# Polysketch attention and hash routing on one core: an earlier end of the early class, gathers ahead of the last x, and a last group in column parts

## The chip, the core and the metric

The kernel runs on one core of one Trainium2 chip. The metric is device microseconds of one execution. The kernel before took 229.28 us as the median of three runs (229.06 to 229.42).

## What is computed

An attention block is followed by a mixture of experts, whose expert for each row follows from the row's token id. All data are float32.

```
q, k, v: (4 batches, 4 heads, 1088 positions, 32);  S1, S2: (8, 32)
phi(x)  = outer product of S1 x and S2 x, 64 features
kv      = sum over positions of phi(k) outer v;   z = sum of phi(k)
attn    = (phi(q) kv) / (phi(q) z + 1e-6)
x       = attn, rows (batch, position), 4352 rows of 4 * 32 = 128
expert  = token_id * 2654435761 mod 8
out     = relu(x w1[expert]) w2[expert],  w1: (8, 128, 1024), w2: (8, 1024, 128)
```

## The kernel before

**Attention, one batch after another.** In a batch, the first 1024 positions are laid out as 128 partitions by T = 8 positions; the last 64 of each batch are handled as tails, all batches together. For batch b, TensorE (PE) transposes k (`transposed`), multiplies by the sketches (`k_products`, `q_products`), and sums kv over the positions (`kv_products`). VectorE (DVE) forms the features: `k_features` (tile kp) from the copied products ab, and `q_features` (tiles f, then fT, its transposed form) in two halves of four positions each, g = 0 and 1. ScalarE (ACT) copies products out of PSUM (`copied`) and puts kv into a block-diagonal matrix m with 16 small copies (`kv_diagonal`, L383). `x_products` multiplies the q features by m in eight groups of matmuls per half, and ACT copies the result to xe. `x_tail_products` does the same for the tail. `denominators` and `x_rows` divide: the main rows on GpSimd (POOL) mostly, one half of one batch on DVE. SyncE (SP) then stores the rows to a scratch tensor x_rows in DRAM, a main store and a tail store for each batch. The loop is skewed: in turn b, the products and kp of batch b + 1 are made between kv and x of batch b, and k of batch b + 2 is transposed.

**The routing**, spread over the turns on DVE: `route_counts` and `route_ranks` count rows for each expert, `route_slots` gives each row its slot, `route_rows` and `route_tiles` make one-hot matrices (row, in_tile, tiles; one half of tiles is made on POOL, L286), and `route_list` and `route_end` turn them, by 34 small matmuls into one PSUM tile, into the row lists `get` and `put`. Each expert has two classes of GN = 288 slots. The early class takes the first 288 rows of the expert among rows 0 to NE - 1, where NE covers the first EB = 3 batches (3264 rows); the late class takes the rest of the expert's rows. What exceeds both classes is done by a loop at the end, whose number of turns is read from n_over.

**The experts**, in 16 groups (8 early, then 8 late) of 288 slots. `bring` gathers tiles of 128 rows by indirect DMA on POOL (L537; six buffers xg), transposes them on PE three at a time, and copies them to xT. `layer1` (L601) has eight matmuls of 288 columns per group, each copied out with a relu by ACT and DVE in turn; `layer2` (L609) has eight, which add up, and runs one group behind. `send` transposes results back and scatters them by indirect DMA on POOL (L542). A gather of an early tile reads only rows below NE, so it waits for the stores of those rows only.

**What sets the order.** Through attention the order on every engine is the order of the program text (`manual_schedule`), up to `ordered.close()`. After it a scheduler places the instructions. In both parts each engine works its list in order. An issued gather waits on POOL, and what stands behind it on POOL waits too. In the last turn of attention before, ten matmuls on constants (`keep_busy(10)`, L157) stand between kv and x:

```python
        if not more:
            keep_busy(10)
        x_products(fTs, m)
        x_tail_products(b, m)
```

The scheduler placed eight gathers ahead of the last batch's x rows on POOL, and `bring` of the first six tiles ahead of the first `layer1`. It placed the last scatter behind the load of n_over and the loop.

Of the kernel before, what the change touches and what calls it, by code (L numbers as in the profile page):

```python
# [24 lines left out]
def kernel(  # L25
# [31 lines left out]
    EB = B - 1  # L57
    NE = EB * S
    EP = NE // C
# [4 lines left out]
    assert E * GN % P == 0 and GN >= P and ST <= P and EP * C == NE and EP % 32 == 0  # L64
# [3 lines left out]
    load = ctx.enter_context(tc.tile_pool(name="load", bufs=2))  # L68
# [27 lines left out]
    def load_main(src, b, tag):  # L96
        t = load.tile([P, H, T, D], F32, tag=tag, name=f"{tag}{b}")
        nc.sync.dma_start(t[:], src[b, :, :SM, :].rearrange("h (p t) d -> p h t d", t=T))
        return t

# [181 lines left out]
    def route_tiles():  # L282
        nc.vector.tensor_tensor(in_tile[:], iota[:, 0:ST].unsqueeze(1).to_broadcast([P, C, ST]),
                                st[:, 0].unsqueeze(2).to_broadcast([P, C, ST]), op=OP.is_equal)
        nc.vector.tensor_scalar(tiles[:, :, 0], in_tile[:], p1[:], None, op0=OP.mult)  # L285
        nc.gpsimd.tensor_tensor(tiles[:, :, 1], in_tile[:], iota[:, 0:C].unsqueeze(2).to_broadcast([P, C, ST]),  # L286
                                op=OP.mult)
# [28 lines left out]
    xe = const.tile([P, GQ * H * Q + H, DA], F32)  # L316
# [21 lines left out]
    def copied(ab_ps, sub):  # L338
        ab = work.tile(list(ab_ps.shape), F32, tag="ab", name="ab")
        nc.scalar.copy(sub(ab), sub(ab_ps))  # L340
        return ab
# [73 lines left out]
    def x_products(fTs, m):  # L415
        for g, fT in enumerate(fTs):
            for h0 in range(0, H, 2):
                p = ps_x.tile([P, 2, Q * DA], F32, tag="x", name="x_ps")
                for h in range(2):
                    for fb in range(FB):  # L420
                        nc.tensor.matmul(p[:, h], fT[:, (h0 + h) * FB + fb],  # L421
                                         m[:, h0 + h, fb].rearrange("p t d -> p (t d)"),
                                         start=(fb == 0), stop=(fb == FB - 1), skip_group_check=True)
                nc.scalar.copy(xe[:, (g * H + h0) * Q:(g * H + h0 + 2) * Q].rearrange("p (h t) d -> p h (t d)", h=2), p[:])  # L424

    def x_tail_products(b, m):
        u, t = b % 2, b // 2
        rows, r = slice(u * SP, (u + 1) * SP), slice(t * D, (t + 1) * D)
        p = ps_x.tile([P, H, DA], F32, tag="x", name="x_ps")
        for h in range(H):  # L430
            for fb in range(FB):
                nc.tensor.matmul(p[rows, h], fT_tail[r, h * FB + fb, rows], m[r, h, fb, t],
                                 start=(fb == 0), stop=(fb == FB - 1), skip_group_check=True,
                                 tile_position=(r.start, rows.start))
        nc.scalar.copy(xe[rows, GQ * H * Q:], p[rows])

    def denominators():
        den = work.tile([P, GQ * H * Q + H], F32, tag="den", name="den")
        nc.vector.tensor_scalar(den[:], xe[:, :, D], 1e-6, None, op0=OP.add)
        nc.vector.reciprocal(den[:], den[:])  # L440
        return den

    def x_rows(b, den):
        u = b % 2
        xs = work.tile([P, T, H, D], F32, tag="xs", name="xs", bufs=1)
        n = H * Q
        for g in range(GQ):
            (nc.vector if b == EB - 1 and g == 0 else nc.gpsimd).tensor_tensor(xs[:, g * Q:(g + 1) * Q].rearrange("p t h d -> p h t d"),  # L448
                                    xe[:, g * n:(g + 1) * n, 0:D].rearrange("p (h t) d -> p h t d", h=H),
                                    den[:, g * n:(g + 1) * n].rearrange("p (h t) -> p h t", h=H).unsqueeze(3)  # L450
                                    .to_broadcast([P, H, Q, D]), op=OP.mult)
        rows = slice(u * SP, (u + 1) * SP)
        xs_tail = work.tile([P, H, D], F32, tag="xs_tail", name="xs_tail", bufs=1)
        nc.gpsimd.tensor_tensor(xs_tail[rows], xe[rows, GQ * n:, 0:D],
                                den[rows, GQ * n:].unsqueeze(2).to_broadcast([SP, H, D]), op=OP.mult)
        nc.sync.dma_start(x_dram[b * S:b * S + SM].rearrange("(p t) d -> p t d", t=T),
                          xs[:].rearrange("p t h d -> p t (h d)"))
        nc.sync.dma_start(x_dram[b * S + SM:(b + 1) * S], xs_tail[rows].rearrange("p h d -> p (h d)"))
# [10 lines left out]
    nc.gpsimd.memset(xe[:, GQ * H * Q:], 1.0)  # L469
# [16 lines left out]
    for b in range(B):  # L486
        more = b + 1 < B
        kv = kv_products(b, (kp, va), (kp_tail, va_tail))
        if more:
            abk_ps = k_products(kTs, T)  # L490
            abq_ps = q_products(qT, T)
            va = values(v_t[b + 1], T, work, "")
# [3 lines left out]
        if b == 1:  # L496
            route_rows(0)
        if b == 2:
            route_tiles()
        m = kv_diagonal(b, kv)  # L500
        if more:
            abk = copied(abk_ps, lambda t: t[:])
            abq = copied(abq_ps, lambda t: t[:])
            kp = k_features(abk, T, work, "")
# [3 lines left out]
        if not more:  # L508
            keep_busy(10)
        x_products(fTs, m)  # L510
        x_tail_products(b, m)
        if b + 2 < B:
            kTs = [transposed(k_t[b + 2], g, Q) for g in range(0, T, Q)]
        den = denominators()
        x_rows(b, den)
        if b == 2:
            route_end(route_list())
        if more:
            fTs = [q_features(abq, 0, slice(0, P), work, "", 2)]
        if b + 2 < B:  # L520
            qT = q_blocks(q_t[b + 2], T)
        if more:
            fTs.append(q_features(abq, 1, slice(0, P), work, "", 2))
        if b == 0:
            load_experts(range(E // 2, E))
            route_slots()
        if b == 1:
            route_rows(1)
    ordered.close()

    hots.release()
    moe = ctx.enter_context(tc.tile_pool(name="moe", bufs=3))

# [6 lines left out]

    def scatter(src, idx):
        st_ = nc.gpsimd.indirect_dma_start(  # L542
            out=out[:], out_offset=bass.IndirectOffsetOnAxis(ap=idx, axis=0),
            in_=src[:], in_offset=None, bounds_check=N - 1, oob_is_err=False)
        tc.declare_no_dep(st_.ins, group="out_rows", reason="distinct rows")
        tc.add_to_no_dep_group("out_rows", st_.ins)
# [14 lines left out]
    def columns(of, name, lo, hi):  # L561
        b = lo // (BT * P)
        if b not in of:
            of[b] = moe.tile([P, BT * P], F32, tag=name, name=name, bufs=2)
        return of[b][:, lo - b * BT * P:hi - b * BT * P]

    done_in = done_out = 0

    def bring(upto):
        nonlocal done_in  # L570
        while done_in < upto:
            n = min(3, ST - done_in)
            xp = ps_x.tile([P, 4, P], F32, tag="x", name="xp")
            for i in range(n):
                xg = moe.tile([P, DM], F32, tag="xg", name="xg", bufs=6)
                gather(xg, get[:, done_in + i:done_in + i + 1], NE if done_in + i < HT else N)
                nc.tensor.transpose(xp[:, i], xg[:], ident[:])  # L577
            evict(done_in // 3, columns(xTs, "xT", done_in * P, (done_in + n) * P),
                  xp[:, 0:n].rearrange("p a b -> p (a b)"))
            done_in += n  # L580

    def send(upto):
        nonlocal done_out
        while done_out + 1 <= upto:
            n = min(2, upto - done_out)
            tp = ps_x.tile([P, 4, P], F32, tag="x", name="tp")
            for i in range(n):
                nc.tensor.transpose(tp[:, i], columns(oTs, "oT", (done_out + i) * P, (done_out + i + 1) * P), ident[:])
# [8 lines left out]
    def layer1(g, c):  # L597
# [3 lines left out]
        nc.tensor.matmul(hp[:], w1[:, g % E, c * P:(c + 1) * P], columns(xTs, "xT", g * GN, (g + 1) * GN), start=True, stop=True)  # L601
# [4 lines left out]
    def layer2(g, c):  # L606
        if c == 0:
            ops[g] = ps_o.tile([P, GN], F32, tag="o", name="op")
        nc.tensor.matmul(ops[g][:], w2[:, g % E, c], hTs[g][:, c], start=(c == 0), stop=(c == FC - 1))  # L609
        if c == FC - 1:  # L610
            nc.scalar.copy(columns(oTs, "oT", g * GN, (g + 1) * GN), ops[g][:])  # L611

    G = 2 * E
    for g in range(G + 1):
        if g < G:
            bring(min(ST, -(-((g + 2) * GN) // P)))
        for c in range(FC):
            if g < G:
                last = layer1(g, c)
            if g > 0:  # L620
                layer2(g - 1, c)
            if c == 3 and g > 1:
                send((g - 1) * GN // P)
    send(ST)
# [4 lines left out]
    with tc.issue_after(last):  # L629
# [22 lines left out]

    w1f = w1[:].rearrange("p e f -> p (e f)")
    w2f = w2[:].rearrange("p e c d -> p (e c d)")
    turns = nc.values_load(n_over[0:1, 0:1], min_val=0, max_val=OT)
    with tc.For_i(0, turns) as j:
# [25 lines left out]
        xg = moe.tile([P, DM], F32, tag="xg", name="xg", bufs=6)  # L682
# [52 lines left out]
```

## Time and profile before

| What | us |
|---|---|
| median of three runs | 229.28 |
| the profiled execution | 229.07 |
| its span | 227.4 |
| PE busy, of the span | 203.9 |
| DVE, POOL, ACT busy | 99.1, 98.0, 70.3 |
| kv of the last batch starts on PE | 61.98 |
| first gather starts on POOL | 69.16 |
| first `layer1` matmul starts | 78.91 |
| last `layer2` matmul ends | 212.56 |
| last scatter starts | 219.61 |

How to read it: the profile is of one execution of the program, and times count from the start of its span. A busy share is no bound in itself: what counts in each stretch is which engine the others wait for. In the page's slices each digit is a tenth of a slice that the engine was busy, and PEclk is the clock that TensorE was granted, in tenths. A timeline line gives start, duration, engine, line, operation, output and inputs, shape, count, and in brackets the idle time before it with what ended it. A matmul of float32 shows as two instructions in its count.

### The profile page before, as it was taken

What the parts mean: (1) busy time and instruction counts of PE and PEld (TensorE: products, weight loads), DVE (VectorE), ACT (ScalarE), POOL (GpSimd) and SP (SyncE); (2) the same over time, 40 slices, a digit from 0 to 9 for tenths busy, and PEclk for the clock granted to TensorE, in tenths of its full rate; (3) what the DMA queues carried; (4) which work ended last, traced back from release to release, by engine and by line L of the source; (5) the groups of instructions that cost most, each with busy time, mean ns of one, the idle gap of its engine ahead of it and who ended that gap; (6) DMA issues with size and microseconds to landing.
All of it is one profiled execution on the core that took longest, in us unless ns stands there. A gap on an engine that the chain in (4) does not pass through costs nothing.

```text
span 227.4 us, 3315 instructions
## 1 busy us (share of the span) xinstructions
PE 203.9 (90%) x1172; PEld 166.1 (73%) x1173; DVE 99.1 (44%) x191; ACT 70.3 (31%) x201; POOL 98.0 (43%) x114
## 2 busy tenths in 40 slices
PE   6799889999799499999999999999999999999400
PEld 2689889999778267777777777777777777777300
DVE  4699568999994132233133212322232232324300
ACT  2243643628235123222331342232223223122100
POOL 4234017044336787046656256566265115213620
PEclk9999999999999769999999999999999999999955
DMA  4999999895021232001111001111011000000000
GB/s 123 286 311 315 314 345 347 288 344 193 3 98 30 53 121 56 16 23 38 46 35 46 23 27 46 46 35 43 19 34 45 0 22 24 15 18 21 30 20 0
DMA packets 22465, 22.16 MB, mean 97 GB/s; under 512 B 5178, under 2 KB 19771, under 8 KB 22448
## 3 DMA queue, kind: packets, MB, share of 16 engines
q1 hardware_dynamic: 17824, 17.05, 23.8%
q0 software_dynamic: 2304, 4.59, 7.0%
q10 hardware_dynamic: 2320, 0.30, 0.8%
q8 instruction: 10, 0.16, 0.3%
q14 instruction: 7, 0.06, 0.1%
HBM read 17.47 MB, written 4.59 MB: 97 GB/s over the span
## 4 chain that ended last, share of the span: by engine, by line
PE 60%; issue 13%; DMA 12%; DVE 5%; POOL 4%; ACT 2%; POOLq 1%; SPq 0%; ACTq 0%
PE hp L601 20%; PE op L609 17%; DMA out_dram<-os,put 8%; PE kv L370 7%; PE ab_ps L333 3%; POOL out_dram L542 2%; PE idle L157 2%; DMA k<-in_k_dram 2%; PE kT_ps L322 2%; PE x_ps L421 2%; PE abq_ps L398 2%; PE xp L577 1%; ACT m L383 1%; POOL xg L537 1%; DVE tiles L285 1%
## 5 line engine op out<-in xcount | busy, mean ns | idle before, releaser
L601 PE MATMUL hp<-xT,w 128*128 128x288 f32 x256 | 84.1, 416 | 0.0
L609 PE MATMUL op<-hT,w 128*128 128x288 f32 x256 | 81.9, 407 | 0.0
L552 DVE TENSOR_SCALAR hT<-hp 128x288 f32<-128x288 f32 x64 | 29.3, 458 | 89.5 <-PE hp L601 86.5
L542 POOL DMA_INDIRECT out_dram<-os,put x36 | 35.8, 993 | 59.1 <-ACT os L550 28.4
L609 PEld LDWEIGHTS op<-hT,w 128*128 128x128 f32 x256 | 48.7, 190 | 13.2
L601 PEld LDWEIGHTS hp<-xT,w 128*128 128x128 f32 x256 | 48.2, 196 | 11.5
L550 ACT ACTIVATE hT<-hp 128x288 f32<-128x288 f32 x64 | 26.3, 410 | 66.3 <-PE hp L601 62.1
L537 POOL DMA_INDIRECT xg<-x_rows,get x36 | 36.7, 1020 | 20.9 <-PE xp L577 8.7
L448 POOL TENSOR_TENSOR xs<-xe,den 128x512 f32<-128x512 f32 x7 | 9.2, 1335 | 24.1 <-DVE den L440 20.9
L383 ACT COPY m<-kv 32x66 f32<-32x66 f32 x64 | 13.2, 206 | 18.3 <-PE kv L370 17.5
L421 PE MATMUL x_ps<-m,fT 128*128 128x132 f32 x128 | 16.1, 281 | 1.5 <-ACT xe L424 1.1
L421 PEld LDWEIGHTS x_ps<-m,fT 128*128 128x128 f32 x128 | 15.0, 190 | 2.3 <-ACT xe L424 1.3
L370 PEld LDWEIGHTS kv<-va,kp 128*128 128x128 f32 x128 | 14.7, 192 | 0.4 <-issue 0.3
L370 PE MATMUL kv<-va,kp 128*128 128x66 f32 x128 | 14.9, 275 | 0.0
L611 ACT COPY oT<-op 128x288 f32<-128x288 f32 x16 | 6.4, 398 | 19.4 <-PE op L609 19.4
L412 DVE STREAM_TRANSPOSE fT<-f 128x1024 f32<-128x1024 f32 (+1 forms) x9 | 11.2, 1244 | 1.0 <-DVE f L345 0.5
L157 PE MATMUL idle<-warm 128*128 128x512 bf16 x31 | 9.8, 442 | 1.4 <-POOL warm L129 1.4
L345 DVE TENSOR_TENSOR f<-ab 128x1024 f32<-128x1024 f32 (+1 forms) x9 | 10.8, 1199 | 0.6 <-ACT ab L340 0.5
L345 DVE TENSOR_TENSOR kp<-ab 128x1024 f32<-128x1024 f32 x8 | 9.4, 1230 | 2.4 <-ACT ab L340 2.4
L577 PE MATMUL xp<-ident,xg 128*128 128x128 f32 x36 | 7.1, 290 | 3.1 <-DMA xg<-x_rows,get 1.7
L333 PE MATMUL ab_ps<-s_k,kT 128*128 128x64 f32 (+1 forms) x72 | 9.2, 277 | 0.7 <-issue 0.7
L333 PEld LDWEIGHTS ab_ps<-s_k,kT 128*128 128x128 f32 (+1 forms) x72 | 8.5, 191 | 1.6 <-issue 1.4
(133 smaller groups left out, 149.2 us busy)
## 6 DMA issues: line engine op xcount, KB each, us to landing
w<-in_moe_w_dram SPq DMA_DIRECT2D x16, 512.0 KB, 7.7
k<-in_k_dram SPq DMA_DIRECT2D x4, 512.0 KB, 4.9
q<-in_q_dram SPq DMA_DIRECT2D x4, 512.0 KB, 5.9
v<-in_v_dram SPq DMA_DIRECT2D x4, 512.0 KB, 6.3
x_rows<-xs SPq DMA_DIRECT2D x4, 512.0 KB, 4.5
xg<-x_rows,get POOLq DMA_INDIRECT x36
out_dram<-os,put POOLq DMA_INDIRECT x36
k_tail<-in_k_dram ACTq DMA_DIRECT2D x4, 32.0 KB, 5.0
```

What stands on the lines that cost most here:

```text
L157: nc.tensor.matmul(p[:], warm[:, 0:P], warm[:], start=True, stop=True)
L333: nc.tensor.matmul(ab_ps[:, g:g + w, h].rearrange("p t x r -> p t (x r)"), kT[:w * D, h], s_k[:w * D, 0:w].rearrange("p t x r -> p (t x r) ...
L345: eng.tensor_tensor(dst, ab[:, :, 0].unsqueeze(3).to_broadcast(shape), ab[:, :, 1].unsqueeze(2).to_broadcast(shape), op=OP.mult)
L370: nc.tensor.matmul(kv[:, pr], kp[rows, t, 2 * pr:2 * pr + 2].rearrange("p h i j -> p (h i j)"), va[rows, t, 2 * pr:2 * pr + 2].rearrange(" ...
L383: nc.scalar.copy(m[t * D:(t + 1) * D, h::2, f, t], src)
L421: nc.tensor.matmul(p[:, h], fT[:, (h0 + h) * FB + fb], m[:, h0 + h, fb].rearrange("p t d -> p (t d)"), start=(fb == 0), stop=(fb == FB - 1 ...
L537: nc.gpsimd.indirect_dma_start(out=dst[:], out_offset=None, in_=x_dram[0:rows], in_offset=bass.IndirectOffsetOnAxis(ap=idx, axis=0), bound ...
L542: st_ = nc.gpsimd.indirect_dma_start(out=out[:], out_offset=bass.IndirectOffsetOnAxis(ap=idx, axis=0), in_=src[:], in_offset=None, bounds_ ...
L550: nc.scalar.activation(dst, src, AF.Relu if relu else AF.Copy)
L552: return nc.vector.tensor_scalar(dst, src, 0.0, None, op0=OP.max).ins
L601: nc.tensor.matmul(hp[:], w1[:, g % E, c * P:(c + 1) * P], columns(xTs, "xT", g * GN, (g + 1) * GN), start=True, stop=True)
L609: nc.tensor.matmul(ops[g][:], w2[:, g % E, c], hTs[g][:, c], start=(c == 0), stop=(c == FC - 1))
```

## The change

1. The early class ends within batch 2: EB is 2, and NE is 2686, the two first batches and most of the first 512 rows of the third. q of that batch is loaded in two parts of 512 positions, so that each half g of it makes 512 neighbouring rows, which are stored by a DMA of their own.
2. The last two batches are written out of the loop. The list (`route_list`) comes before x of batch 2, whose first half (g = 0) stands before kv of batch 3 and whose second half and tail stand behind it. Six gathers are issued on POOL before x of batch 3, three more by the scheduler. Only three tiles are transposed ahead of the first `layer1`; `bring` moves behind the fourth matmul of each group. xe has two buffers, ab three, and xg and xT lie in a pool of their own, so that they exist before attention ends. `keep_busy(10)` is gone.
3. `route_slots` moves to turn 0, ahead of kp; `route_rows` follows x of turns 0 and 1; both halves of tiles are made on DVE. All x rows of batch 2 are made on DVE, those of batch 3 on POOL.
4. The last group's `layer2` runs as two column parts (160 and 128), with a `send` behind each. The tables of the overflow loop are made after group 12, and a barrier of the scheduler stands ahead of the loop: in the built order, the last scatter stands ahead of the load of n_over.

```diff
-    EB = B - 1
-    NE = EB * S
-    EP = NE // C
+    EB = B - 2
+    EP = (EB * S + SM // 2) // C
+    NE = EP * C
...
-        nc.gpsimd.tensor_tensor(tiles[:, :, 1], in_tile[:], iota[:, 0:C].unsqueeze(2).to_broadcast([P, C, ST]),
+        nc.vector.tensor_tensor(tiles[:, :, 1], in_tile[:], iota[:, 0:C].unsqueeze(2).to_broadcast([P, C, ST]),
...
+    b, e = EB, EB + 1
+    kv = kv_products(b, (kp, va), (kp_tail, va_tail))
+    abk_ps = k_products(kTs, T)
+    abq_ps = q_products(qT, T)
+    va = values(v_t[e], T, work, "")
+    m = kv_diagonal(b, kv)
+    abk, abq2 = copied(abk_ps, lambda t: t[:]), copied(abq_ps, lambda t: t[:])
+    kp = k_features(abk, T, work, "")
+    idx = route_list()
+    x_products(b, 0, fTs[0], m)
+    route_end(idx)
+    kv = kv_products(e, (kp, va), (kp_tail, va_tail))
+    denominators(b, 0, HQ)
+    x_main(b, 0, nc.vector)
+    fetch(3)
+    fTs.append(features_of(abq, 1))
+    x_products(b, 1, fTs[1], m)
+    x_tail_products(b, m)
+    fetch(6)
+    fTs = [features_of(abq2, 0), features_of(abq2, 1)]
+    m = kv_diagonal(e, kv)
+    denominators(b, HQ, GQ * HQ + H)
+    x_main(b, 1, nc.vector)
+    x_tail(b, nc.vector)
+    for g in range(GQ):
+        x_products(e, g, fTs[g], m)
+    bring(3)
+    x_tail_products(e, m)
+    denominators(e, 0, GQ * HQ + H)
+    for g in range(GQ):
+        x_main(e, g, nc.gpsimd)
+    x_tail(e, nc.gpsimd)
...
-    for g in range(G + 1):
-        if g < G:
-            bring(min(ST, -(-((g + 2) * GN) // P)))
+    for g in range(G):
         for c in range(FC):
-            if g < G:
-                last = layer1(g, c)
+            last = layer1(g, c)
             if g > 0:
                 layer2(g - 1, c)
+            if c == 3:
+                bring(min(ST, -(-((g + 2) * GN) // P)))
             if c == 3 and g > 1:
                 send((g - 1) * GN // P)
-    send(ST)
+        if g == G - 4:
+            tables_after = last
+    send((G - 1) * GN // P)
+    for lo, hi in ((0, GN - P), (GN - P, GN)):
+        for c in range(FC):
+            layer2(G - 1, c, lo, hi)
+        send(ST - 1 if hi < GN else ST)
...
+    tc.no_sync_barrier()
```

`fetch(n)` issues the gathers up to tile n; `x_main` and `x_tail` are the two parts of the former `x_rows`.

## Prediction

> **What bounds the kernel now.** First the page's slices: TensorE (PE) is nearly full from the third slice (5.685 us each) on, except for one dip with a lower granted clock, and the last third of slice 38 onwards.
>
> ```profile
> PE   6799889999799499999999999999999999999400
> PEclk9999999999999769999999999999999999999955
> ```
>
> From 85.5 us to 207.8 us PE is full with the expert layers (L601 and L609, one matmul each 0.485 us, 20.00 us busy in each stretch of 20). The change leaves that work alone: 16 groups of 8 + 8 matmuls, 36 transposes in, 36 out. So time can come from two places only: the passage from attention to the layers, and the tail. The timeline of PE in the passage:
>
> ```profile
> 65.67 0.66 PE L370 MATMUL kv<-va_tail,kp_tail 64*128 64x66 f32 x4
> 66.26 2.33 PE L157 MATMUL idle<-warm 128*128 128x512 bf16 x10
> ...
> 73.05 1.11 PE L432 MATMUL x_ps<-m,fT 32*64 32x33 f32 x16
> 74.09 0.44 PE L577 MATMUL xp<-ident,xg 128*128 128x128 f32 x2
> ...
> 78.65 0.47 PE L577 MATMUL xp<-ident,xg 128*128 128x128 f32 x1 [0.69 <-DMA xg<-x_rows,get]
> ```
>
> Attention ends on PE at 74.1. Then six gathered tiles are transposed one by one as they land, and the first layer matmul starts at 78.91. The gathers, 1.3 us apart on GpSimd (POOL), started only at 69.16, when x of batch 2 (issued at 65.23 and 65.65) had landed. The same passage in windows (busy PE, granted clock, DMA share, GB/s):
>
> ```profile
> 66.16:69.57 3.41, 3.37 (x18) 1.00 0.40 148
> 69.57:72.99 3.42, 3.07 (x26) 1.00 0.15 41
> 72.99:76.40 3.41, 2.13 (x22) 0.99 0.14 38
> 76.40:79.81 3.41, 1.67 (x5) 0.50 0.24 58
> 79.81:83.22 3.41, 3.41 (x9) 0.51 0.28 97
> ```
>
> The waiting also cost the clock: half speed from 76.4 to 83.2. Group 0's eight matmuls took 6.16 us (78.91 to 85.07) instead of 8 x 0.485 = 3.88. Last, POOL's timeline at the end:
>
> ```profile
> 214.18 0.98 POOL L542 DMA_INDIRECT out_dram<-os,put  x1 [0.41 <-issue]
> 215.46 0.98 POOL L542 DMA_INDIRECT out_dram<-os,put  x1 [0.30 <-issue]
> 219.61 0.98 POOL L542 DMA_INDIRECT out_dram<-os,put  x1 [3.16 <-issue]
> ```
>
> The last scatter starts 3.16 us after the one before it ended: in the built order it stands behind the load of n_over, the barrier that waits for all DMAs, and the loop of zero turns.
>
> **The early class ends sooner.** NE goes from 3264 to 2686 rows. From the token ids, the smallest expert still has 297 early rows, over the 288 slots, so every early slot stays full, no overflow turn appears, and the layers' work is the same. A gather of the early class now needs batch 2's first 512 rows only.
>
> **Upstream, batches 0 to 2.** VectorE (DVE) sets the pace there: 15.72 us busy in 46 to 62. I follow it with durations of the trace.
> - The 16 slot operations (39.65 to 43.17, 3.5 us) move into batch 0, behind rank (23.33) and ahead of kp. DVE was idle there for 2.37 + 0.51 us, and the third ab buffer lets the tail copy of ab (28.17, behind kp) go at 26.2. So: slots to 26.9, tail f and fT to 29.4, kp to 31.8. kv of batch 1 starts at about 31.5 instead of 33.15. Behind kp stand row (2.4), den, f, fT, qT: qT is ready at 38.4 instead of 36.85, and q_products start at 38.5 (39.19 before). Batch 1 thus runs 0.7 us ahead; kv of batch 2 starts at 46.2 (46.91).
> - In batch 2 DVE does den to 46.3, f, fT, qT to 50.0, in_tile to 51.4, then both halves of tiles. The second was POOL's. The trace has 2.62 us for DVE's half beside POOL's 2.25; a DVE row of the same size is in_tile, 1.42. Bounds for both halves: 2.0 to 4.9 us. The Trainium skill (GPSIMD Engine Reference, "Key points") says that GpSimd shares its SBUF interfaces with VectorE, and names DVE instructions in a 2-port mode or with two SBUF inputs as those that collide. The trace agrees for the first (DVE's half ended at 60.73, just after POOL's at 60.40) and not for the second (f took 1.16 beside POOL's xs, 1.22 alone). By the row alone the pair costs 2.62 + 1.42 = 4.0; by the rule the first half shrinks once POOL is quiet. POOL copies va until about 52.4, so I take 3.2: tiles ready at 54.6. PE is done with q_products at 54.1.
> - PE then does the list (1.26) to 55.9 and x of batch 2's first half. Its second pair shares one PSUM buffer with the first, as the list holds the other: 0.9 + 0.8 + 0.9 to 58.5. DVE: kp of batch 3 to 57.0, list arithmetic (1.55 before, with a stretched 0.72; I take 1.1) to 58.1, then it waits for ACT's copy (59.25), den 0.4, x rows 0.69: 60.4. kv of batch 3 fills PE from 58.5 to 62.6, which hides this.
>
> **First gathers.** SP issues the half x at 60.45; nothing late stands before it on SP (the expert loads ended at 46.5, now about 1.4 later). The whole x needed 3.9 us to release a gather; half of it 3 to 3.9. First gather at 63.4 to 64.4, against 69.16; third tile landed (two steps of 1.3, 0.4 for the longer first, 2.6) by 69.5. The loads of q in halves (descriptors half as long) were landed long before use, so they cost nothing.
>
> **Last x.** DVE: f, fT of batch 2's second half to 62.9; PE x 62.95 to 64.8, tail to 65.9. ACT copies the tail to 66.45 and only then starts m of batch 3 (16 copies, 3.5 us): m is queued behind these copies though kv ended at 62.6. So m ends at 70.0; before it ended at 69.87. Here nothing is won. x of batch 3 follows from 70.0 to 73.15 (69.92 to 73.05 before), three transposes without a wait (0.35), tail (1.05), first layer matmul at 75.1 to 75.5: I say 75.3 against 78.91. The other three transposes stand inside group 0 with their tiles landed by 73.4. POOL's next three gathers wait for the first transposes, and the last x rows (2.1 + 0.4) stand behind them; they end near 80 as before (82.2), needed only by the late class.
>
> **The removed idle matmuls.** The ten (2.33 us) covered m's copies. Now PE has 65.9 to 70.0 with four x instructions. The Trainium skill (TensorE: Matmul & The Clock Gate, "HAM oscillation — how this bites in real kernels") asks for no PE gap over about 3.4 us, since an idle window halves the clock. That speaks against the change. The trace agrees: drops at 76.40 and, after the end of work, near 216.35, which is 41 steps of 3.413 apart, and the return 6.8 after the first. If the grid lies as here, 66.16 to 69.57 is nearly empty and the clock is halved from 69.57 to 72.99. x of batch 3 then ends 1.5 us later. By the rule 1.5 (bounds 0.6 to 3.4 by where the grid lies); by the row of 72.99 to 76.40 alone, which fell with 2.13 us busy, as likely. I take 1.5.
>
> **Sum of the passage.** Group 0 with its and the next group's transposes ended at 85.5. Now 75.3 + 3.88 + 0.7 = 79.9, plus 1.5 for the clock: 81.4. Gain 4.1.
>
> **Tail.** The last group in columns of 160 and 128: an instruction of 288 columns takes 0.2425 us, so one of 160 takes 0.135; kv's (66 columns, 32 in 3.65 us) show 0.114 as a floor, which I take for 128. So 16 x 0.135 + 16 x 0.114 = 3.98 us against 3.88, plus two waits for oT copies (0.4 and 0.35). But tiles 31 to 34 leave from 210.2, 1.28 us apart; tile 35 goes fifth at 215.3, where tile 34 went at 215.46. In the built order it now stands ahead of n_over. What followed the barrier stays; the scatter behind it goes. It costs at least its 0.98 us and at most 0.98 + 2.26 (its landing, as 215.46 to 217.72): I take 2.3, as the end came long after its landing. The table operations move four groups up on DVE, which is a quarter busy there: nothing.
>
> Sum: 4.1 + 2.3 = 6.4. The profiled run took 229.07 (span 227.4, and 1.67 around it): 222.7. The median of 229.28 stands 0.2 over it, within their spread.
>
> **Rivals.**
> - The clock never drops, because the four instructions and the tails count as activity or the grid lies otherwise: 221.2. Against it: 72.99 to 76.40 was busier and fell.
> - The passage is lengthened on DVE (4.9 us for tiles, 1.7 later) or the clock stays low for two windows, 1.9 more: 224.4 to 226.3. For it: DVE is full in batch 2.
> - The early gathers do not come early (a wait on later x rows): then only the tail is won, about 227 to 229. Against it: the first gather waits for three x stores, up to the first half.
> - Slower: without idle matmuls the clock stays halved into the layers. A window at half speed costs 1.7 us; to eat 6.4 + 0.46 it must last four windows beyond the one counted. The point from which it decides is 86.6 us: still halved then, it is slower. Against it: 79.81 to 83.22, full at half speed, brought the clock back. About 230 to 232.
>
> **Numbers.** Forecast 0.50 (221.9 to 223.8), no drop 0.20, lengthened 0.19, not early 0.05, slower 0.06. The first three are all faster, and most of the fourth: faster 0.92, same 0.02, slower 0.06, with 0.2% as what a measurement here can tell from no change. Range 220.7 to 225.6.
>
> **What would show it.** First gather near 64; m of the last batch starting right after the tail copy, near 66.5; first L601-type matmul near 75 to 77; a clock of 0.50 for one window from about 69.6; layers full from there; no scatter behind the barrier, and the end 5 to 7.5 us after the last landing. I am wrong if kp or tiles of batch 2 come over a microsecond late, if PE waits for gathered tiles, or if the end moves less than the start of the layers does.

## The result, and the profile after

| us | before | after |
|---|---|---|
| median, run together (4 runs each) | 229.35 | 222.88 |
| the profiled execution | 229.07 | 222.88 |
| its span | 227.4 | 221.2 |
| kv tail of the last batch starts on PE | 65.67 | 60.77 |
| first gather starts on POOL | 69.16 | 61.98 |
| first `layer1` matmul | 78.91 | 75.63 |
| first `layer2` matmul | 85.99 | 80.43 |
| last `layer1` matmul | 207.32 | 202.54 |
| last scatter | 219.61 | 210.50 |

The ratio is 0.967, with a 95% interval of 0.958 to 0.977; one of the four runs of after, 225.5 us at a mean clock of 0.952, and one of before, 231.9, were in a slower state and are left out of it. The forecast was 222.7. Of the span's 6.2 us, 4.78 are there when the last `layer1` matmul starts, and 1.42 are won behind it (20.08 us from there to the end before, 18.66 after).

The slices of the page after (5.53 us each) still show one dip in PE with a lower clock, now in slices 12 and 13:

```profile
PE   7799999999979999999999999999999999999700
PEclk9999999999995899999999999999999999999975
```

PE's timeline in the passage after. L429 is the x products, L440 their tail, L378 kv, L582 the transposes of gathered tiles, L654 `layer1`:

```profile
60.77 0.66 PE L378 MATMUL kv<-va_tail,kp_tail 64*128 64x66 f32 x4
61.55 2.07 PE L429 MATMUL x_ps<-m,fT 128*128 128x132 f32 x16
63.55 1.11 PE L440 MATMUL x_ps<-m,fT 32*64 32x33 f32 x16
65.82 0.49 PE L429 MATMUL x_ps<-m,fT 128*128 128x132 f32 x2 [1.16 <-ACT m L391]
66.70 7.37 PE L429 MATMUL x_ps<-m,fT 128*128 128x132 f32 x30 [0.39 <-ACT m L391]
73.90 0.49 PE L582 MATMUL xp<-ident,xg 128*128 128x128 f32 x3
74.59 1.11 PE L440 MATMUL x_ps<-m,fT 32*64 32x33 f32 x16 [0.20 <-ACT xe L432]
75.63 2.21 PE L654 MATMUL hp<-xT,w 128*128 128x288 f32 x8
```

Three gathered tiles are transposed without a wait for a DMA: the gathers are no longer in the way. What is left are the copies of m (ACT, 64.92 to 68.43) and an x of batch 3 that takes from 68.48 to 73.90, 5.42 us, where before it took 3.13. The windows say why (busy PE, granted clock, DMA share, GB/s):

```profile
63.30:66.70 3.40, 1.85 (x22) 0.98 0.13 41
66.70:70.10 3.40, 3.24 (x11) 0.50 0.44 141
70.10:73.50 3.40, 3.40 (x18) 0.51 0.08 23
73.50:76.90 3.40, 3.20 (x29) 1.00 0.08 19
```

The clock is halved for two windows, from 66.6 to 73.4, not for one as forecast. At the end, POOL's timeline has the last scatter 0.31 us behind the one before it, where 3.16 us lay between them:

```profile
209.21 0.98 POOL L629 DMA_INDIRECT out_dram<-os,put  x1 [0.30 <-issue]
210.50 0.98 POOL L629 DMA_INDIRECT out_dram<-os,put  x1 [0.31 <-issue]
```

### The profile page after: what moved, and what is told of

It reads as the page before. It is cut to its first block, busy times and chain, and to the rows that moved or that the text cites. A ratio compares the mean times of both kernels' runs of the same rounds, so it can differ in the third digit from the quotient of the medians.

```text
span 221.2 us, 3345 instructions
## 1 busy us (share of the span) xinstructions
PE 203.1 (92%) x1178; PEld 167.6 (76%) x1179; DVE 99.8 (45%) x196; ACT 70.5 (32%) x202; POOL 94.1 (43%) x112
## 4 chain that ended last, share of the span: by engine, by line
PE 49%; DVE 20%; DMA 11%; issue 10%; POOL 2%; ACT 2%; SPq 1%; DVEq 0%; POOLq 0%; ACTq 0%
PE hp L654 21%; PE op L662 20%; DMA out_dram<-os,put 8%; PE x_ps L429 4%; DVE f L353 4%; DVE fT L420 3%; DMA q<-in_q_dram 3%; DVE qT L397 2%; DVE kp L353 2%; DVE row L287 2%; POOL out_dram L629 2%; ACT m L391 1%; PE xp L582 1%; PE tp L641 1%; PE x_ps L440 1%
## 5 line engine op out<-in xcount | busy, mean ns | idle before, releaser
L662 PE MATMUL op<-hT,w 128*128 128x288 f32 (+2 forms) x272 | 82.1, 392 | 0.0
L654 PE MATMUL hp<-xT,w 128*128 128x288 f32 x256 | 82.0, 407 | 0.0
L662 PEld LDWEIGHTS op<-hT,w 128*128 128x128 f32 x272 | 49.8, 191 | 12.4
L654 PEld LDWEIGHTS hp<-xT,w 128*128 128x128 f32 x256 | 47.3, 190 | 11.7
L429 PE MATMUL x_ps<-m,fT 128*128 128x132 f32 x128 | 19.8, 314 | 2.4 <-ACT m L391 1.5
L429 PEld LDWEIGHTS x_ps<-m,fT 128*128 128x128 f32 x128 | 17.9, 219 | 3.7 <-ACT m L391 2.6
L459 POOL TENSOR_TENSOR xs<-xe,den 128x512 f32<-128x512 f32 x6 | 7.7, 1299 | 19.9 <-DVE den L454 12.1
L378 PEld LDWEIGHTS kv<-va,kp 128*128 128x128 f32 x128 | 14.7, 192 | 0.1
L378 PE MATMUL kv<-va,kp 128*128 128x66 f32 x128 | 14.7, 273 | 0.0
L664 ACT COPY oT<-op 128x288 f32<-128x288 f32 (+2 forms) x17 | 6.6, 385 | 18.8 <-PE op L662 18.8
L432 ACT COPY xe<-x_ps 128x264 f32<-128x264 f32 x16 | 6.1, 379 | 17.0 <-PE x_ps L429 17.0
L165 PE MATMUL idle<-warm 128*128 128x512 bf16 x21 | 7.7, 484 | 1.4 <-POOL warm L137 1.4
```

The costliest lines, as they stand in the source:

```text
L378: nc.tensor.matmul(kv[:, pr], kp[rows, t, 2 * pr:2 * pr + 2].rearrange("p h i j -> p (h i j)"), va[rows, t, 2 * pr:2 * pr + 2].rearrange(" ...
L429: nc.tensor.matmul(p[:, h], fT[:, (h0 + h) * FB + fb], m[:, h0 + h, fb].rearrange("p t d -> p (t d)"), start=(fb == 0), stop=(fb == FB - 1 ...
L662: nc.tensor.matmul(ops[g][:, 0:hi - lo], w2[:, g % E, c], hTs[g][:, c, lo:hi], start=(c == 0), stop=(c == FC - 1))
```

## The experiments

The profiled runs are compared by stretches that start at a common event, since before itself took 229.35, 230.41, 230.56 and 229.6 us (medians) on the chips of the four groups of runs. "Passage" is the time from the kv tail of the last batch to the first `layer1` matmul, "tail" that from the last `layer1` matmul to the end of the span. Each ratio is against runs of before on the same chip. In the next table the stretches are those of the one profiled run of each kernel; the medians are of all its runs, taken on different chips, so that kernels are compared by the ratio and not by the median.

| kernel | passage | kv tail to first `layer2` | tail | median | ratio (interval) |
|---|---|---|---|---|---|
| before | 13.24 | 20.32 | 20.08 | 229.35 | |
| after | 14.86 | 19.66 | 18.66 | 222.88 | 0.967 (0.958-0.977) |
| idle matmuls back | 12.48 | 17.28 | 19.0 | 221.96 | 0.968 (0.959-0.976) |
| m first | 12.76 | 17.56 | 19.1 | 222.7 | 0.968 (0.956-0.979) |
| m first, idle | 12.53 | | | 221.93 | 0.967 (0.963-0.971) |
| before, no idle matmuls | 13.21 | 20.78 | | 230.19 | 0.998 (0.995-1.002) |
| whole early class | 17.35 | 24.67 | | 229.16 | 0.997 (0.994-0.999) |
| slots late | 14.94 | 19.74 | | 227.12 | 0.988 (0.984-0.992) |
| half of tiles on POOL | 14.20 | 19.00 | | 224.44 | 0.977 (0.972-0.982) |
| last scatter behind the loop | | | 20.34 | 225.96 | 0.981 (0.974-0.988) |
| last group whole | | | 19.63 | 224.99 | 0.977 (0.973-0.982) |
| before, with the barrier | 13.19 | | 19.71 | 229.56 | 0.996 (0.993-0.999) |

Three things were at issue. The first is the clock: the theory is that the gap left by the idle matmuls costs the passage 2 us and more, the rival that m's copies set x of batch 3 and cover it. The second is the earlier start: is it the early end of the class, the place of the slots, or the half of tiles that brings it? The third is the tail: is it the scatter's place, the column parts, or neither, since the end waits for something else?

A reader may wonder that the passage itself grew, from 13.24 to 14.86: it starts 4.9 us sooner, because x of batch 2 no longer stands whole ahead of kv of batch 3.

### Idle matmuls back

Twelve matmuls on constants between the tail of x(2) and x(3), where PE had nothing to do:

```diff
     x_main(b, 1, nc.vector)
     x_tail(b, nc.vector)
+    keep_busy(12)
     for g in range(GQ):
```

> The changed kernel with twelve idle matmuls on constants (2.8 us at full clock) between the tail of batch 2's x and x of batch 3 on PE. Theory A (the gap on PE while ACT makes m of the last batch halves the clock, and that lengthens x of batch 3): the clock stays at 1.00 through the passage, the 26 x matmuls after m take 3.1 to 3.2 us and not 5.4, the first layer matmul starts near 73.4 and not 75.63, the time falls by 2.2 to about 220.6. Theory B (the layers' start is set by the gathers or by ACT's copies, and the clock only fills a wait): first layer matmul near 75.6, time within 0.5 of 222.9.

PE's windows in this kernel, the same stretch as above:

```profile
64.40:67.80 3.40, 3.40 (x29) 1.00 0.17 41
67.80:71.20 3.40, 3.00 (x23) 1.00 0.47 141
71.20:74.60 3.40, 3.20 (x34) 1.00 0.09 23
```

The clock stays at 1.00, x(3) takes 3.08 us from the last copy of m, and the passage is 12.48 us instead of 14.86: 2.4 us. So the gap that the removed idle matmuls left is what lowers the clock, and that costs 2.4 us in this place, not 1.5. Three of its four runs had a mean granted clock of 0.980 to 0.982 and took 221.85 to 222.0 us; the fourth had 0.962 and took 224.25. The four of after had 0.952 to 0.972. The time of 220.6 that was expected did not come: in the profiled run the kv tail of the last batch stood 1.04 us later than in after (61.81 against 60.77), ahead of the edit, and the tail of the kernel took 0.34 us more, and with 2.38 won in the passage this is the span of 220.2. The two ratios, 0.968 and 0.967, are the same, so that the passage is faster is shown by one profiled run, and a gain of the whole kernel is not measured.

### m of the last batch first

The 16 copies of m go ahead of ACT's copies of x(2)'s second half. That takes away what m is queued behind:

```diff
     fetch(3)
+    m2 = kv_diagonal(e, kv)
     fTs.append(features_of(abq, 1))
     x_products(b, 1, fTs[1], m)
     x_tail_products(b, m)
...
-    m = kv_diagonal(e, kv)
+    m = m2
```

> The changed kernel with the 16 copies of m of batch 3 put on ACT ahead of the x copies of batch 2's second half and tail. Theory A (m queued behind these copies is what makes PE wait from 64.7 to 68.5): m from 61.2 to 64.8, x of batch 3 from about 66.4 to 69.6 at full clock (the gap on PE, 63.6 to 65.3, is too short to halve it), first layer matmul near 71.2, time 218.4. Theory B (gathers set the start; the third tile lands near 68 to 69.5): first layer matmul not before 71 as well, but with a wait of transposes on DMA and little more than the 2.2 us of the clock gained: 220.5.

PE's timeline and windows of this kernel:

```profile
61.50 2.07 PE L429 MATMUL x_ps<-m,fT 128*128 128x132 f32 x16
65.33 1.11 PE L440 MATMUL x_ps<-m,fT 32*64 32x33 f32 x16 [1.76 <-ACT xe L432]
66.37 5.53 PE L429 MATMUL x_ps<-m,fT 128*128 128x132 f32 x32
```

```profile
63.40:66.75 3.35, 1.59 (x21) 0.99 0.16 42
66.75:70.00 3.25, 3.25 (x17) 0.50 0.43 136
70.00:73.40 3.40, 3.21 (x35) 0.98 0.13 34
```

m is done at 64.87 instead of 68.43, and x(3) starts 2.1 us sooner. But x(2)'s tail now waits 1.76 us for an x buffer in PSUM, which ACT empties only behind m, and the clock fell again, for one window. x(3) takes 5.4 us, as in after: ACT's copies of its first two parts are 1.76 us apart at half clock, those of the last two 0.9, so that the clock costs 1.7. The passage is 12.76: the 2.1 of the earlier start are won, and what a full clock would add is not. The 218.4 us that were expected did not come. Its runs spread widely: 221.15 and 221.2, then 224.19 and 225.32 at mean clocks of 0.955 and 0.952.

### m first, and idle matmuls

Both edits together, with `keep_busy(7)` between x(2)'s second half and its tail.

> The changed kernel with m of batch 3 ahead of the x copies of batch 2's second half on ACT, and seven idle matmuls on PE between that second half and the tail. Theory D (a stretch of 3.4 us with about half of it idle is enough to halve the clock, so that the earlier m without idle matmuls won only what the shorter gap is worth): with them the clock stays at 1.00, x of batch 3 takes 3.2 us, first layer matmul 2.2 us sooner than with the earlier m alone and 4.3 sooner than in the changed kernel (counted from the tail of the last kv), time 218.5 to 219.5. Rival (gathers set the start): the third tile lands near 68.0 and PE waits for it; no more than 1 us gained over the earlier m alone.

PE's timeline of this kernel:

```profile
69.61 2.07 PE L429 MATMUL x_ps<-m,fT 128*128 128x132 f32 x16
72.04 1.17 PE L429 MATMUL x_ps<-m,fT 128*128 128x132 f32 x8 [0.36 <-ACT xe L432]
73.50 1.17 PE L429 MATMUL x_ps<-m,fT 128*128 128x132 f32 x8 [0.29 <-ACT xe L432]
```

The clock held in the passage, at 12.53 us, no better than with idle matmuls alone, and the 218.5 to 219.5 us expected did not come. x(3) now starts 5.67 us behind the kv tail instead of 7.7, but takes 5.3 us at full clock: PE waits for ACT to empty x buffers. ACT's first copy of x(3) came about 1.2 us later than PE was done with it; why is not settled. In the profiled run the clock fell elsewhere, from 38.5 to 45.35, in batch 1, though PE was busy for 3.24 of the 3.40 us before the drop: 223.84 us at a mean clock of 0.963. Why it fell there is open. PE's windows around it (busy PE, granted clock, DMA share, GB/s):

```profile
35.10:38.50 3.40, 3.24 (x27) 1.00 1.06 333
38.50:41.90 3.40, 3.40 (x18) 0.50 0.97 317
```

The runs of this kernel fall into two groups by their clock, 223.64 and 223.84 at 0.963 to 0.964, and 221.34 to 222.08 at 0.979 to 0.981.

### The kernel before without its idle matmuls

```diff
         if not more:
-            keep_busy(10)
+            pass
```

> The kernel before without its ten idle matmuls. If they do hold the clock: without them it falls to 0.50 near 69 to 70, x of the last batch ends 1.5 to 3 us later (near 76), still ahead of the sixth tile (78.65); the first layer matmul stays near 78.9 to 79.5, but the clock is back sooner, so group 0 may take down to 3.9 us instead of 6.16: 227 to 229.5. If they hold nothing (four x matmuls in the gap are enough activity): clock 1.00 until after 73, time 229.3.

```profile
68.50:71.90 3.40, 2.46 (x10) 0.53 0.04 10
71.90:75.30 3.40, 3.40 (x17) 0.50 0.23 58
75.30:78.70 3.40, 3.03 (x30) 0.97 0.17 41
```

The same drop that the change has, and here it is free: the windows of half clock moved ahead of group 0 (its eight matmuls took 4.05 us instead of 6.16), the passage is 13.21 instead of 13.24, and then, behind group 0, a transpose waits 2.64 us for a gather. The ratio is 0.998. In the kernel before the gathers ended last, so that the idle matmuls were worth nothing there; in the changed kernel the gathers are early, and such matmuls are worth 2.4 us (the passage of the first experiment).

### The early class over three whole batches

NE is 3264 again, with the split x of batch 2 kept, and the gathers are issued behind all of that x:

```diff
-    EP = (EB * S + SM // 2) // C
+    EP = (B - 1) * S // C
...
-    fetch(3)
...
-    fetch(6)
...
     x_tail(b, nc.vector)
+    fetch(6)
```

> The changed kernel with an early class over all 3264 rows of three batches again, and so the six gathers issued behind all x rows of batch 2. Theory A (the early end of the class brings the first gathers forward by some 6 us, which the layers' start needs): first gather near 71.9, third tile landed near 77.3, first layer matmul near 78.5, clock low once more in the layers: 225.7 to 227.5. Rival (three tiles instead of six ahead of the first layer matmul are what helped): first layer matmul within 1 us of 75.6, time within 1 of 222.9.

POOL's timeline and PE's timeline of this kernel:

```profile
72.52 1.23 POOL L542 DMA_INDIRECT xg<-x_rows,get  x1 [19.44 <-issue]
```

```profile
76.74 0.33 PE L582 MATMUL xp<-ident,xg 128*128 128x128 f32 x1 [0.83 <-DMA xg<-x_rows,get]
77.97 0.33 PE L582 MATMUL xp<-ident,xg 128*128 128x128 f32 x1 [0.90 <-DMA xg<-x_rows,get]
79.55 3.54 PE L653 MATMUL hp<-xT,w 128*128 128x288 f32 x8
```

Group 0 starts 17.35 us behind the kv tail instead of 14.86, and the first `layer2` comes 5.0 us later. Nearly all of the change's gain is gone (0.997). This is more than was expected, and it is more than the worth of the earlier end alone: with x(2) split around kv(3), rows of its second half are stored later than they were before, so the first gather came 10.3 us behind the kv tail, against 3.5 before and 1.2 in the change. The clock has its share too: it fell a second time, from 78.88 to 82.29, under the first layer matmuls. This run moved the end of the class and the place of the gathers together; the split order needs the early end, and what the early end is worth in the order of before was not run.

### Slots late

`route_slots` back behind batch 0, `route_rows` as before; the rest as changed.

```diff
-            route_slots()
+        if b == 1:
+            route_rows(0)
...
-        route_rows(b)
...
+        if b == 0:
+            route_slots()
+    route_rows(1)
```

> The changed kernel with the slots and the two row matrices on DVE where the kernel before has them: slots at the end of turn 0, rows early in turn 1 and ahead of tiles. Theory A (the move of the slots into DVE's idle time of batch 0 brings the list forward): kv of batch 1 may start up to 0.8 sooner, but tiles are ready 1.5 to 2.4 us later and with them the first layer matmul; time 224.4 to 225.3. Rival (DVE has room elsewhere, the place of the slots is indifferent): within 0.5 of the changed kernel, counted from the first kv to the first layer matmul.

DVE's timeline, then PE's, of this kernel:

```profile
27.18 1.22 DVE L353 TENSOR_TENSOR f<-ab 64x1024 f32<-64x1024 f32 x1 [3.16 <-ACT ab L348]
...
52.91 2.27 DVE L291 TENSOR_TENSOR in_tile<-iota,st 128x1224 bf16<-128x1224 f32 x1
55.21 0.54 DVE L293 TENSOR_SCALAR tiles<-in_tile,p 128x1224 bf16<-128x1224 bf16 x1
```

```profile
57.15 1.82 PE L300 MATMUL idx_ps<-tiles,row 128*128 128x72 bf16 x34 [3.39 <-DVE tiles L294]
```

DVE idles 3.16 us in batch 0, and the slots stand in the full part of its day. `route_ranks`, ahead of the edit, ended at 24.02 here and at 23.00 in after, so times count from there: tiles are ready 33.1 us behind it, against 30.3. PE then waits 3.39 us, loses its clock from 57.5 to 61.0, and the kv tail comes 41.4 us behind that point instead of 37.8. So the step of the prediction that filled DVE's idle time is confirmed, and is worth 3.6 us: 2.8 at the tiles, the rest behind them, where the clock fell. Part of the 2.8 is no fault of the slots themselves: in_tile took 2.27 us beside POOL's copy of va, and 1.39 in after. The passage still had its own drop (71.25 to 78).

### One half of tiles on POOL again

```diff
-        nc.vector.tensor_tensor(tiles[:, :, 1], in_tile[:], ...
+        nc.gpsimd.tensor_tensor(tiles[:, :, 1], in_tile[:], ...
```

This kernel was recorded twice, the first time with a single run:

> The changed kernel with the second half of tiles on GpSimd again. By the shared interface: DVE's half lasts until GpSimd is done, 2.2 to 2.6 us instead of 1.20, both halves ready near 53.9 instead of 53.3, and the list on PE starts 0.6 later; kp hardly moves. If nothing collides: DVE's half 1.2 us, GpSimd's 1.2 to 2.3 behind its copy of va (51.6), ready near 53.9 too. So time within 0.7 of the changed kernel, and the durations tell the two apart.

It took 232.62 us, with the clock halved from 38.3 to 45.2, from 62.2 to 72.5 and from 75.9 to 82.7, so its time tells nothing of the tiles. In its order of work the list stood in the same place behind kv(2) as in after, within 0.5 us. With four runs:

> Again the changed kernel with the second half of tiles on GpSimd, whose one run had lost its clock. Seen there: DVE's half 0.54, GpSimd's 2.53, the list as late after kv of batch 2 as in the changed kernel; but the list copy waits and a later second pair of x leaves PE idle near 59. Theory: the clock falls earlier, near 62, and for longer; 224 to 227. Rival (that run was disturbed as a whole): within 0.7 of 222.9.

DVE's timeline, then POOL's:

```profile
51.03 0.54 DVE L293 TENSOR_SCALAR tiles<-in_tile,p 128x1224 bf16<-128x1224 bf16 x1
53.85 3.08 DVE L353 TENSOR_TENSOR kp<-ab 128x1024 f32<-128x1024 f32 x2 [2.28 <-ACT ab L348]
```

```profile
51.14 2.53 POOL L294 TENSOR_TENSOR tiles<-in_tile,iota 128x1224 bf16<-128x1224 bf16 x1 [1.55 <-DVE in_tile L291]
53.67 1.03 POOL L368 COPY va<-v 128x1024 f32<-128x1024 f32 x1
```

The pair takes 2.6 to 2.7 us from in_tile either way, so that the tiles are ready at the same time. What follows is later: POOL's copy of va now lies on kp, which took 3.08 instead of 2.36; the list arithmetic on DVE follows it, and the second pair of x(2)'s first half waits for that: it starts 12.35 us behind the start of kv(2), 1.3 later than in after (56.15 less 45.13 is 11.02). Three of the four runs took 223.8 to 224.97; the fourth took 232.49 at a mean clock of 0.930, nearly the same as the single run, so the long loss of the clock came in two of five runs, and why is open. The intervals of the ratios overlap, so a worth of this edit in the whole kernel is not measured. What the trace shows is that moving the half gains nothing at the tiles, and some 1.3 us behind them, since kp stays clear of POOL's copy.

### The last scatter behind the loop again

```diff
-    tc.no_sync_barrier()
```

> The changed kernel without the barrier of the scheduler ahead of the overflow loop, so that the last scatter stands behind the loop again. As predicted on record, the scatter behind the loop costs 2.3 us less the nothing that it costs ahead: 225.2. Theory C (after the result: before, 11.94 us passed from the last scatter ahead of the loop to the end, afterwards 10.7; the scatter moved ahead takes 1.28 on POOL and the one behind takes 1.24, so the move is worth nothing): within 0.3 of 222.9, the end 11.9 to 12.0 us after the last scatter ahead of the loop.

```profile
210.62 0.98 POOL L629 DMA_INDIRECT out_dram<-os,put  x1 [0.30 <-issue]
216.56 0.98 POOL L629 DMA_INDIRECT out_dram<-os,put  x1 [4.95 <-issue]
```

The tail is 20.34 us instead of 18.66: 1.7. The theory that the scatter is free, since the end waits for other things, is wrong: within 0.3 of 222.9 was its forecast, and the runs took 225.11 to 226.29.

### The last group whole

The barrier stays, and the last `layer2` runs once over 288 columns:

```diff
-    for lo, hi in ((0, GN - P), (GN - P, GN)):
+    for lo, hi in ((0, GN),):
```

> The changed kernel with the last group's second layer whole (288 columns) and its three tiles sent together. As predicted on record, the column parts are worth 0.1. Theory C (the tail's whole gain is that tiles 33 and 34 leave 1.5 us sooner after the last first-layer matmul): last scatter 1.2 to 1.6 us later after it (near 9.4 instead of 7.96), the time 224.2.

```profile
212.04 0.99 POOL L629 DMA_INDIRECT out_dram<-os,put  x1 [0.30 <-issue]
213.33 0.98 POOL L629 DMA_INDIRECT out_dram<-os,put  x1 [0.30 <-issue]
```

The last scatter goes 9.66 us behind the last `layer1`, instead of 7.96. The tail is 19.63: the column parts are worth 1.0 us, 0.7 less than they bring the scatter forward. They can bring it forward only because a smaller edit comes with them: `send` of tiles 31 and 32 now stands ahead of the last `layer2`, so that tile 31 leaves 2.80 us behind the last `layer1` here and in after, against 4.18 before, and the five scatters of after follow each other every 1.29 us from there. That edit, and the move of the overflow tables, were not taken back alone.

### The kernel before, with the barrier

```diff
+    tc.no_sync_barrier()
     w1f = w1[:].rearrange("p e f -> p (e f)")
```

> The kernel before with only the barrier ahead of the overflow loop added, so that the last scatter stands ahead of it. As predicted on record: 2.3 gained behind the loop and 1.28 spent ahead, 228.3. Theory C: the last scatter at 216.7, the end 10.7 later, time within 0.3 of 229.3.

The tail is 19.71 us instead of 20.08, and the ratio 0.996: with the last group whole, the barrier alone wins 0.4 in the profiled run. Not all of the scatters kept their places: the barrier also put more of the overflow tables on DVE ahead of the copy that tile 31 needs, and tile 31 left 4.63 us behind the last `layer1`, against 4.18.

## Why the prediction was right

The time came out as forecast, 222.88 against 222.7, and by the mechanism forecast in the main: earlier gathers, a shorter way to the first layer matmul, and no scatter behind the loop. But two sizes in the sum were off by almost the same amount in opposite directions, and the drop of the clock came a window early and lasted two.

**First gathers.** Half of x was issued at 59.11 (60.45 forecast) and released a gather 2.87 us later (3 to 3.9). The first gather at 61.98 is 1.4 us sooner than the early end of the forecast. No tile was waited for. The rival that the gathers do not come early falls.

**Upstream of x(3).** Each step stood where the prediction put it, and a little sooner: slots ended at 26.47 (26.9), q of batch 2 was laid out at 37.5 (38.4), kv(2) started at 45.13 (46.2), tiles were ready at 53.31 (54.6), m(3) started at 64.92 (66.5), x(3) went on at 68.48 (70.0). Of those 1.5 us, 0.4 are there at the end of rank already (22.92 against 23.33), which no edit touches. Another 0.66 is the pair of tiles, costed at 3.2 and measured at 2.54. Here a reading of the prediction was wrong. It took DVE's 2.62 us beside POOL for work that is slowed. The half takes 0.54 by itself, and the rest was a wait. The Trainium skill (SBUF — State Buffer, "SBUF: two separate sides") calls the port pair of VectorE and GpSimd an exclusive lock, which the first to start holds for its whole instruction while the other blocks. The rows agree: 0.54 where DVE started 0.11 us before POOL, 1.20 beside the end of POOL's copy of va, 2.62 where the two halves started within 0.04 us of each other and DVE's ended 0.33 us behind POOL's, 2.27 instead of 1.39 for in_tile where POOL held the copy first. The prediction's own counterexample, f with 1.16 beside POOL's xs, is of the same kind: f had started first, and POOL's two xs took 2.75 beside it and 2.06 with DVE mostly idle. In the pair of 2.62 us DVE's record starts first, by 0.04 us, and yet it waited, so which of the two holds the ports when they start that close is not told by the trace.

**m behind x(2)'s copies.** m(3) started right after the tail copy, as said, and ended at 68.43. The reading that ACT's queue and not kv sets m is shown by the run that moved it: 3.5 us sooner.

**The clock.** The drop came in the gap that was forecast, but at 66.6 and not at 69.6, behind a window that was busy for 1.85 of 3.40 us and not empty. The rule that the prediction took from the skill, on gaps of over 3.4 us, did not hold as it stands, since no gap on PE there was longer than 1.16 us; the row of before that fell with 2.13 us busy was the better guide. Where the window lies was taken from the grid of one trace, and it lies 0.4 us later in after and elsewhere again in other runs: that a drop came is mechanism, that its cost was near is in part luck. The term was under-sized: one window and 1.5 us in the sum, two windows and 2.3 to 2.4 us on the chip (x(3) at 5.42 against 3.13; the passage with idle matmuls 2.38 shorter). The upper bound of 3.4 held it. The rival with no drop at all was real in the run that filled the gap; as a forecast of this kernel it was wrong. The rival in which the clock stays halved into the layers fell: the clock was back at 73.5, 13 us before the point at which it decided.

**The sum of the passage.** Group 0 with its transposes ended at 79.95 (80.43, less one matmul of 0.485), against 81.4 forecast: 5.56 us sooner than before, not 4.1. Between there and the last `layer1`, after needs 0.78 us more than before: 0.33 for the three tiles that are now transposed behind that point (three take 0.33, as from 77.67 to 78.00), and 0.45 not traced. What stays is 4.78.

**The tail.** This is the step that failed in size: 2.3 forecast for the scatter behind the barrier, 1.42 measured for the whole tail. Tile 35 left 7.96 us behind the last `layer1` (7.98 by the forecast's 215.3), so its place was right. What the sum left out is when scatters land. The trace's line on the scatters of after:

```profile
DMA to landing us min/median/max: 2.2/2.3/4.0
```

The 4.0 is tile 34's, and tile 35's took 2.9. With that the tails add up. From the last `layer1` to the landing of the last scatter ahead of the loop, before took 8.14 + 2.26 = 10.4, and after 7.96 + 2.9 = 10.86. From there to the end of the span, before took 9.7 us, with a scatter behind the loop (217.7 to 227.4), and after 7.8 without one (213.4 to 221.2; also 7.8 with the last group whole, if its last scatter lands 2.2 us after its start, as most do), just over the 5 to 7.5 us that the prediction named. So the late scatter cost 1.9, less than the 2.3 taken and within the bounds of 0.98 and 3.24, and 0.46 of it is given back by the later landing: 1.44.

It also explains why the two edits need each other. With the last group whole, the scatter that moves ahead of the loop starts 1.29 us behind its forerunner, all of them start 0.35 us later than before, and the barrier wins 0.4 (1.9 less 1.64 would be 0.3). With column parts, tile 34 lands as late as 4.0 after its start, tile 35 only 0.2 later, and the barrier wins 1.7. The column parts win 1.0 with the barrier, and the tail is 0.26 longer without it than before (20.34 against 20.08, all other edits of the tail in place), where the late landing of tile 34 holds the loop.

The sum on the chip: 4.78 + 1.42 = 6.2, for 4.1 + 2.3 = 6.4. What is won ahead of the tail was forecast 0.7 too low, and the tail 0.9 too high. That the total fits so closely is partly luck.

## What to carry to other kernels

Idle matmuls that hold the clock are worth something only where PE's own work ends last in the stretch behind them: in the kernel before they bought nothing, and the change that brought the gathers forward made them worth 2.4 us in the same edit that removed them. So ask again of each such prop after the bound has moved. At the end of a kernel count from the landing of the last transfer, not from its issue: a store issued 1.7 us sooner landed only 1.0 us sooner (with 2.2 us taken for the landing of the other), and that was the gain.

## What the runs showed of the hardware

- The clock falls on less than an idle window. It fell behind windows with 2.13 of 3.41 us busy (before), 1.85 of 3.40 (after) and 1.59 of 3.35 (m first, with one gap of 1.76 us and 32-row matmuls for much of the rest). The window with 3.00 us busy in the run with idle matmuls kept it. The skill's rule (TensorE: Matmul & The Clock Gate, "HAM oscillation — how this bites in real kernels") speaks of gaps over some 3.4 us; in before and after no gap in the window was longer than 1.2 us. The busy share is not the whole rule: with m first and idle matmuls the clock fell behind a window with 3.24 of 3.40 us busy, and in the single run with half of tiles on POOL behind one with 2.99. What sets it off there is open.
- The place and the length of the drop are not fixed by the kernel: with m first and idle matmuls, a drop of two windows stood in batch 1 in the profiled run, while four other runs had mean clocks of 0.98 and so most likely no such drop. With it goes the time, by about 2 us: 221.7 against 223.7 us, the means of its two groups of runs. Differences under 1% between such kernels need the granted clock of each run beside its time.
- Two scatters issued 1.29 us apart land in 2.2 to 2.3 us mostly, but with column parts the fourth of the last five took 4.0 to 4.5 us in the four kernels whose landings were read (after, idle matmuls back, m first, last scatter behind the loop), and the fifth 2.9 to 3.4 where it followed at once. With the last group whole the trace gives no landings. The cause is open.
